# First products of a two-layer network by Strassen's method over pairs of token blocks, weights streamed from DRAM

## The chip, the cores and the metric

The kernel runs on one core of one Trainium2 chip. The metric is device time in microseconds of one execution; less is better. Engine names are those of the profile: PE (TensorE matmul) with PEld (its weight loads), DVE (VectorE), ACT (ScalarE), POOL (GpSimd), SP (SyncE, which here issues every DMA).

## What is computed

Linear attention with an RMS norm gives 4,608 tokens of width 512. Two feed-forward layers follow, each 512 to 2,048 to 512, the first with a scaled squared ReLU, the second with x·sigmoid(1.702x):

```
kv = einsum('bhsd,bhse->bhde', k, v)
out = einsum('bhsd,bhde->bhse', q, kv)
out = out / sqrt(mean(out * out, axis=-1) + 1e-06) * g_norm
x = out.transpose(0, 2, 1, 3).reshape(4608, 512)
h = x @ w1_in;  x = (s * max(h, 0)**2 + b) @ w1_out
h = x @ w2_in;  return (h / (1 + exp(-1.702 * h))) @ w2_out
```

Weights come as float64 and are rebuilt as float32 on the chip. Every large product is made of three float32r matmuls: an operand is split into a high part (`hi`, `gh`, `xh`) and the rest (`lo`, `gl`, `xl`), and high×high, high×low and low×high are summed.

## The kernel before

Tokens stand in nine blocks `j` of 512, the hidden width in sixteen slices `f` of 128, and the layers are `m` = 0 and 1. A step (m, j, f) is two batches of 12 matmuls of 512 columns: `mlp_h` (L255) makes the hidden slice `h` from all 512 inputs, and `mlp_o` (L295), one step later, adds the slice's share to four output banks `o`. Between them `mlp_act` (L263 to L267) and `mlp_g` (L275 to L279) turn `h` into `gh` and `gl` on ACT and DVE. There are 2·9·16 = 288 steps.

Everything else is side work with a due time, called a slot: slot 2i is the `mlp_h` of step i and slot 2i+1 its `mlp_o`, so one slot is one batch of 12 matmuls. The lists at the end of the kernel give each side function its slot: loading and converting weights (`w_load`, `w_low`, `w_words`, `w_hi`, `w_lo`, L82 to L116), the key-value products (`kv_product`, L149, L150), and the attention of the next block (`att_product` L182, `att_mean` L198, `att_newton` L208 to L210, `att_split`). The engines take their instructions in exactly this order. All weights of a layer, high and low, stay in SBUF; those of the second layer are converted during the last block of the first and the first of the second, into the same tiles. PSUM's eight banks are four `o`, two `h` (which the key-value products share) and two for attention.

Of the kernel before, what the change touches and what calls it, by code (L numbers as in the profile page):

```python
# [13 lines left out]
P = 128  # L14
# [13 lines left out]
CONV = [(0, 1, 2, 3), (-0.5, 0, 1, 1.5), (0, 1, 2.5, 4.5)]  # L28
# [3 lines left out]
def kernel(ctx: ExitStack, tc: tile.TileContext, qT, kv_h, kvt, cst,  # L32
# [43 lines left out]
    conv, W = {}, {}  # L76

    def w_load(m, f, which):
        raw = wp.tile([P, 512, 2], U32, tag=f"w{which}_{f}", name="raw")
# [8 lines left out]
        conv[m, f, which] = raw  # L88

    def w_low(m, f, which):  # L90
        raw = conv[m, f, which]
        q = tp.tile([P, 512], U32, tag="ca", name="ca", bufs=4)
        u = tp.tile([P, 512], U32, tag="cu", name="cu", bufs=2)
        act.activation(q, raw[:, :, 0], AF.Copy, scale=2.0 ** -29)
        act.activation(u.bitcast(F32), raw[:, :, 1].bitcast(F32), AF.Abs)
        conv[m, f, which] = (raw, q, u)

    def w_words(m, f, which):
        raw, q, u = conv[m, f, which]
        uf = u.bitcast(F32)  # L100
        dve.tensor_scalar(out=uf, in0=uf, scalar1=ABS_MIN, scalar2=ABS_MAX, op0=ALU.max, op1=ALU.min)  # L101
        dve.tensor_scalar(out=u, in0=u, scalar1=3, scalar2=0x3FFFFFFF, op0=ALU.logical_shift_left, op1=ALU.bitwise_and)  # L102
        dve.scalar_tensor_tensor(out=u, in0=raw[:, :, 1], scalar=SIGN_TOP, in1=u, op0=ALU.bitwise_and, op1=ALU.bitwise_or)  # L103
        dve.tensor_tensor(out=q, in0=u, in1=q, op=ALU.add)  # L104
        conv[m, f, which] = q

    def w_hi(m, f, which):
        a = conv[m, f, which]
        w = wp.tile([P, 2, 512], F32R, tag=f"w{which}_{f}", name=f"w{which}_{f}")
        W[m, f, which] = (w[:, 0, :], w[:, 1, :])  # L110
        act.activation(w[:, 0, :], a.bitcast(F32), AF.Copy)

    def w_lo(m, f, which):
        a = conv.pop((m, f, which))
        hi, lo = W[m, f, which]
        dve.tensor_sub(out=lo, in0=a.bitcast(F32), in1=hi.bitcast(F32))  # L116
# [3 lines left out]
    kvd = [dp.tile([P, NP, D], F32, name=f"kvd{b}") for b in range(B)]  # L120

    def kv_load(b, p):
        if b == 0 and p >= 2:
            t = xp.tile([P, 2, 8, P], F32, tag=("xh", "xl")[p % 2], name="kv_in")
        else:
            t = kp.tile([P, 2, 5, P], F32, tag="kv", name="kv_in")
        nc.sync.dma_start(out=t[:, :, 0:4, :], in_=kv_h[b, p])
        nc.sync.dma_start(out=t[0:D, :, 4, :], in_=kvt[b, p])
        kvin[b, p] = t
# [8 lines left out]
    def q_load(j, p):  # L138
        where = (sp, "s") if j == 0 and p >= 2 else (kp, "q")
        qq = where[0].tile([P, T], F32, tag=where[1], name="qq")  # L140
        for o, n, b, s in segments(j):
            nc.sync.dma_start(out=qq[:, o:o + n], in_=qT[b, p, :, s:s + n])
        qin[j, p] = qq

    def kv_product(b, p, where):
        t = kvin.pop((b, p))
        kv = where[0].tile([P, T], F32, tag=where[1], name="kv")
        for c in range(4):
            pe.matmul(kv[:, :P], lhsT=t[:, 0, c, :], rhs=t[:, 1, c, :], start=(c == 0), stop=False)  # L149
        pe.matmul(kv[:, :P], lhsT=t[0:D, 0, 4, :], rhs=t[0:D, 1, 4, :], start=False, stop=True)  # L150
# [10 lines left out]
        dve.tensor_copy(out=hi, in_=kv[D:P, D:P])  # L161
        if b == 0:
            done.add(("kv", b, p))
# [13 lines left out]
    def att_product(j, p, where):  # L177
        qq = qin.pop((j, p))
        assert all(("kv", b, p) in done for _, _, b, _ in segments(j))
        o_ps = where[0].tile([P, T], F32, tag=where[1], name="o_ps")  # L180
        for o, n, b, s in segments(j):
            pe.matmul(o_ps[:, o:o + n], lhsT=kvbd[b % 2][:, p, :], rhs=qq[:, o:o + n], start=True, stop=True)  # L182
        sq = tp.tile([P, T], F32, tag="t", name="sq")
# [4 lines left out]
        sh = tp.tile([P, T], F32R, tag="t", name="sh")  # L188
        sl = tp.tile([P, T], F32R, tag="t", name="sl")
        act.activation(sh, sq, AF.Copy)  # L190
        dve.tensor_sub(out=sl, in0=sq, in1=sh.bitcast(F32))
        att[j, p] = (o_ps, ones, (sh, sl))

    def att_mean(j, p, where):
        o_ps, mat, parts = att[j, p]
        ms = where[0].tile([P, T], F32, tag=where[1], name="ms")
        for n, sq in enumerate(parts):
            pe.matmul(ms, lhsT=mat, rhs=sq, start=(n == 0), stop=(n == len(parts) - 1))  # L198
        y = tp.tile([P, T], F32, tag="t", name="y")
        y2 = tp.tile([P, T], F32, tag="t", name="y2")  # L200
# [5 lines left out]
    def att_newton(j, p):  # L206
# [3 lines left out]
        dve.scalar_tensor_tensor(out=y2, in0=o_ps, scalar=g_col, in1=y, op0=ALU.mult, op1=ALU.mult)  # L210
        att[j, p] = y2

    def att_split(j, p):
        x = att.pop((j, p))
        if p == 0:
            xT[0, j] = (xp.tile([P, NP, T], F32R, tag="xh", name="xh"), xp.tile([P, NP, T], F32R, tag="xl", name="xl"))
        xh, xl = xT[0, j]
        if j:
            act.activation(xh[:, p, :], x, AF.Copy)  # L219
        else:  # L220
            dve.tensor_copy(out=xh[:, p, :], in_=x)
        pool.tensor_sub(out=xl[:, p, :], in0=x, in1=xh[:, p, :].bitcast(F32))  # L222
# [3 lines left out]
    x2d = [dp.tile([NP, P, T], F32, name=f"x2d{j}") for j in range(NB)]  # L226
    x2in = {}

    def x2_load(j, p):
        t = sp.tile([P, T], F32, tag="s", name="x2")  # L230
        nc.sync.dma_start(out=t, in_=x2d[j][p])
        x2in[j, p] = t

    def x2_split(j, p):
        if p == 0:
            xT[1, j] = (xp.tile([P, NP, T], F32R, tag="xh", name="xh"), xp.tile([P, NP, T], F32R, tag="xl", name="xl"))
        xh, xl = xT[1, j]
        t = x2in.pop((j, p))
        act.activation(xh[:, p, :], t, AF.Copy)  # L239
        pool.tensor_sub(out=xl[:, p, :], in0=t, in1=xh[:, p, :].bitcast(F32))  # L240
        done.add((1, j, p))
# [4 lines left out]
    def mlp_h(m, j, f):  # L246
        xh, xl = xT[m, j]
        wh, wl = W[m, f, 0]
        assert all((m, j, c) in done for c in range(NP))
        h = ps_h.tile([P, T], F32, tag="h", name="h")  # L250
        n = 0
        for c in range(NP):
            cc = slice(c * P, (c + 1) * P)
            for a, x in ((wh, xh), (wh, xl), (wl, xh)):
                pe.matmul(h, lhsT=a[:, cc], rhs=x[:, c, :], start=(n == 0), stop=(n == 3 * NP - 1))  # L255
                n += 1
        G[m, j, f] = h

    def mlp_act(m, j, f):
        h = G[m, j, f]  # L260
        r = gp.tile([P, T], F32, tag="r", name="r")
# [6 lines left out]
        G[m, j, f] = r  # L268

    def mlp_g(m, j, f):  # L270
        r = G[m, j, f]
        gh = gp.tile([P, T], F32R, tag="gh", name="gh")
        gl = gp.tile([P, T], F32R, tag="gl", name="gl")
# [6 lines left out]
        G[m, j, f] = (gh, gl)  # L280

    def mlp_o(m, j, f):
        gh, gl = G.pop((m, j, f))
        wh, wl = W[m, f, 1]
        if f == 0:
            acc[m, j] = [ps_o.tile([P, T], F32, tag=f"o{c}", name=f"o{c}") for c in range(NP)]
        for c in range(NP):
            o = acc[m, j][c]
            cc = slice(c * P, (c + 1) * P)
            if m == 0:  # L290
                pairs = ((wh[:, cc], gh), (wh[:, cc], gl), (wl[:, cc], gh))
            else:
                pairs = ((gh[:, cc], wh), (gh[:, cc], wl), (gl[:, cc], wh))
            for n, (a, x) in enumerate(pairs):
                pe.matmul(o, lhsT=a, rhs=x, start=(f == 0 and n == 0), stop=(f == NF - 1 and n == 2))  # L295

    def mlp_store(m, j):
        for c in range(NP):
            o = acc[m, j][c]
            t = sp.tile([P, T], F32, tag="s", name="st")  # L300
            if c % 2:
                dve.tensor_copy(out=t, in_=o)
            else:
                act.activation(t, o, AF.Copy)
            if m == 0:
                nc.sync.dma_start(out=x2d[j][c], in_=t)
            else:
                nc.sync.dma_start(out=out[j * T + c * P:j * T + (c + 1) * P, :], in_=t)

# [126 lines left out]
```

## Time and profile before

| | |
|---|---|
| median of 3 runs | 1712.54 us (1711.75 to 1712.58) |
| the profiled execution: device time, span of its instructions | 1712.43 us, 1710.6 us |
| PE, DVE, ACT busy in the span | 1685.7 us, 721.9 us, 745.7 us |
| matmuls of PE in the built program | 7,214, of which 3,456 in `mlp_h`, 3,456 in `mlp_o` |
| bytes moved by DMA | 93.22 MB |

Busy time is the sum of an engine's instruction records, and overlapping records of one engine count once. A matmul's record is longer than its pitch, because matmuls are pipelined; the pitch is read from the chain of waits, where a batch is listed with its length. A wait is put down to what came last.

### The profile page before, as it was taken

The page shows a single profiled execution, that of the slowest core. Times are in us where ns is not written, and L with a number is a line of the kernel's source. Part 1 is how long each engine was busy: PE and PEld are TensorE (multiplying, and loading weights), DVE is VectorE, ACT ScalarE, POOL GpSimd, SP SyncE. Part 2 cuts the span into 40 slices and gives each one's busy share as a digit, 9 for nine tenths or more (in the row PEclk, how much of TensorE's full clock was granted, in tenths as well). Part 3 has the DMA queues.
Part 4 walks back from the last instruction along what each step waited for, and adds up shares of the span by engine and source line. Part 5 has one row for each costly group of instructions (what it writes and reads, how often), then busy time and mean ns, then how long its engine had stood idle before and what let it go on. Part 6 is the DMA issues. An engine that isn't in the chain of part 4 may idle for free.

```text
span 1710.6 us, 18774 instructions
## 1 busy us (share of the span) xinstructions
PE 1685.7 (99%) x7460; PEld 1380.0 (81%) x7460; DVE 721.9 (42%) x1110; ACT 745.7 (44%) x1218; POOL 96.1 (6%) x82
## 2 busy tenths in 40 slices
PE   7999999999999999999999999999999999999998
PEld 5877888888888888888877788888888888888887
DVE  5997233433434343434578842222222222222222
ACT  5776455545455454555676532222222222222222
POOL 1000000000000000000000000000000000101000
PEclk8999999999999999999999999999999999999999
DMA  7863401010100001010434110101010101000000
GB/s 239 272 210 104 121 19 46 7 47 7 40 13 32 22 1 53 1 44 7 160 124 164 46 50 1 49 0 48 2 44 7 44 7 38 12 27 24 20 7 25
DMA packets 67655, 93.22 MB, mean 54 GB/s; under 512 B 13808, under 2 KB 40432, under 8 KB 67568
## 3 DMA queue, kind: packets, MB, share of 16 engines
q1 hardware_dynamic: 67568, 92.04, 17.0%
q8 instruction: 58, 0.95, 0.2%
q14 instruction: 29, 0.24, 0.0%
HBM read 72.22 MB, written 19.79 MB: 54 GB/s over the span
## 4 chain that ended last, share of the span: by engine, by line
PE 89%; DVE 7%; DMA 1%; ACT 1%; issue 1%; SPq 0%; DVEq 0%; ACTq 0%
PE o L295 42%; PE h L255 42%; PE o_ps L182 2%; DVE cu L103 1%; PE kv L149 1%; DVE w L116 1%; PE ms L198 1%; DVE ca L104 1%; DVE cu L102 1%; DVE gl L279 1%; DVE cu L101 1%; PE kv L150 1%; DVE r L276 0%; DMA kv_in<-in_kv 0%; DVE r L267 0%
## 5 line engine op out<-in xcount | busy, mean ns | idle before, releaser
L255 PE MATMUL h<-xh,w 128*128 128x512 f32 x2304 | 769.0, 395 | 0.1
L255 PEld LDWEIGHTS h<-xh,w 128*128 128x128 f32 x2304 | 433.2, 188 | 95.0 <-issue 1.7
L255 PE MATMUL h<-xl,w 128*128 128x512 f32 x1152 | 449.0, 390 | 0.0
L295 PE MATMUL o<-gh,w 128*128 128x512 f32 x1152 | 378.2, 389 | 0.0
L295 PE MATMUL o<-w,gh 128*128 128x512 f32 x1152 | 356.2, 390 | 3.4 <-ACT gh L278 3.3
L279 DVE TENSOR_TENSOR gl<-r,gh 128x512 fp32r<-128x512 f32 x288 | 228.9, 795 | 113.6 <-ACT gh L278 100.6
L267 DVE TENSOR_TENSOR r<-h,r 128x512 f32<-128x512 f32 x144 | 99.5, 691 | 414.8 <-ACT r L266 414.8
L266 ACT ACTIVATE r<-h 128x512 f32<-128x512 f32 x144 | 85.8, 596 | 414.8 <-PE h L255 414.7
L295 PEld LDWEIGHTS o<-w,gh 128*128 128x128 f32 x1152 | 216.7, 188 | 49.7 <-ACT gh L278 5.0
L255 PEld LDWEIGHTS h<-xl,w 128*128 128x128 f32 x1152 | 216.8, 188 | 47.7 <-issue 2.7
L295 PEld LDWEIGHTS o<-gh,w 128*128 128x128 f32 x1152 | 216.2, 188 | 45.2 <-ACT gh L275 0.4
L276 DVE TENSOR_SCALAR r<-r,cst_sb 128x512 f32<-128x512 f32 x144 | 78.7, 547 | 379.3 <-ACT gh L275 379.1
L295 PE MATMUL o<-gl,w 128*128 128x512 f32 x576 | 224.9, 390 | 3.7 <-DVE gl L279 3.7
L295 PE MATMUL o<-w,gl 128*128 128x512 f32 x576 | 225.0, 391 | 0.0
L263 ACT ACTIVATE r<-h 128x512 f32<-128x512 f32 x144 | 85.7, 595 | 249.3 <-PE h L255 249.3
L278 ACT ACTIVATE gh<-r 128x512 fp32r<-128x512 f32 x144 | 91.1, 633 | 124.7 <-DVE r L267 124.7
L295 PEld LDWEIGHTS o<-gl,w 128*128 128x128 f32 x576 | 108.1, 188 | 28.8 <-DVE gl L279 6.5
L295 PEld LDWEIGHTS o<-w,gl 128*128 128x128 f32 x576 | 108.3, 188 | 24.1 <-DVE gl L279 1.7
L275 ACT ACTIVATE gh<-r,cst_sb 128x512 fp32r<-128x512 f32 x144 | 117.5, 816 | 4.8
L264 ACT ACTIVATE r<-r 128x512 f32<-128x512 f32 x144 | 91.0, 632 | 4.6
L222 POOL TENSOR_TENSOR xl<-y,xh 128x512 fp32r<-128x512 f32 x36 | 47.6, 1323 | 773.7 <-ACT xh L219 414.0
L240 POOL TENSOR_TENSOR xl<-x,xh 128x512 fp32r<-128x512 f32 x36 | 46.8, 1301 | 698.3 <-ACT xh L239 568.4
(53 smaller groups left out, 846.1 us busy)
## 6 DMA issues: line engine op xcount, KB each, us to landing
raw<-in_w_in SPq DMA_DIRECT2D x32, 512.0 KB, 5.7
kv_in<-in_kv SPq DMA_DIRECT2D x32, 512.0 KB, 4.6
raw<-in_w_out SPq DMA_DIRECT2D x32, 512.0 KB, 6.3
x2d<-st SPq DMA_DIRECT2D x36, 256.0 KB, 2.1
x<-x2d SPq DMA_DIRECT2D x36, 256.0 KB, 2.9
out<-st SPq DMA_DIRECT2D x36, 256.0 KB, 2.1
kv_in<-in_kvt SPq DMA_DIRECT2D x32, 64.0 KB, 4.3
qq<-in_qT SPq DMA_DIRECT2D x8, 256.0 KB, 5.1
```

The costliest lines, as they stand in the source:

```text
L222: pool.tensor_sub(out=xl[:, p, :], in0=x, in1=xh[:, p, :].bitcast(F32))
L240: pool.tensor_sub(out=xl[:, p, :], in0=t, in1=xh[:, p, :].bitcast(F32))
L255: pe.matmul(h, lhsT=a[:, cc], rhs=x[:, c, :], start=(n == 0), stop=(n == 3 * NP - 1))
L263: act.activation(r, h, AF.Relu)
L264: act.activation(r, r, AF.Square)
L266: act.activation(r, h, AF.Sigmoid, scale=1.702)
L267: dve.tensor_mul(out=r, in0=h, in1=r)
L275: act.activation(gh, r, AF.Identity, scale=s_col, bias=b_col)
L276: dve.tensor_scalar(out=r, in0=r, scalar1=s_col, scalar2=b_col, op0=ALU.mult, op1=ALU.add)
L278: act.activation(gh, r, AF.Copy)
L279: dve.tensor_sub(out=gl, in0=r, in1=gh.bitcast(F32))
L295: pe.matmul(o, lhsT=a, rhs=x, start=(f == 0 and n == 0), stop=(f == NF - 1 and n == 2))
```

## The change

Blocks are taken in pairs wherever there are two left: in layer 0, blocks 0 to 2 stay as they were (`plain`), and 3 to 8 form three pairs; in layer 1 blocks 0 to 7 form four pairs and block 8 stays plain. A pair runs in two phases. In the first, `strassen` makes the hidden values of both blocks: for each group `i` of two slices and both halves of the 512 inputs, the 2×2 block product (slices × input halves, by input halves × blocks) is made of seven products of 6 matmuls, in place of eight (two `mlp_h` batches for each of two blocks, 48 matmuls, become 42). In the second phase, `mlp_o` runs as before for both blocks, slice by slice, with eight output banks. The first phase takes 28 slots per pair, and the second 32.

Sums of weight blocks (S1 to S4) are made once per layer (`s_sums`), split, and stored in DRAM (`wsd`) with the plain blocks; both phases load their weights from there (`op_load`, `wo_load`, four slots ahead, `LEAD`). Sums of the inputs are made per pair (`x_operands`) during the second phase before. `g1_sum` joins the seven products, on DVE for five of them. Attention from block 3 on writes its result to DRAM; its units for blocks 5 and 6 stand in the first phase of pair (3, 4), and those of 7 and 8 in that of pair (5, 6). Layer 1's weights are converted in slots 100 to 252, over the three pairs of layer 0. SBUF is 42 slots of 4 KB and 22 of 2 KB per partition, and PSUM eight banks, each given to the next user in the order in which they were freed (`Slots`).

```diff
+NBIG, NMID = 42, 22
+NPLAIN = 3
+LEAD = 4
+OPS = ("A11", "S2", "S3", "S1", "A12", "A22", "S4", "A21")
+PRODUCTS = (("A11", "B11"), ("S2", "T2"), ("S3", "T3"), ("S1", "T1"), ("A12", "B21"), ("A22", "T4"), ("S4", "B22"))
...
+    def op_load(m, i, k):
+        n = min(2, len(PRODUCTS) - 2 * k)
+        t = wl[m, i, k] = new4(F32R, "wl")
+        nc.sync.dma_start(out=t[:, 0:n, :].bitcast(F32), in_=wsd[m][i][:, 2 * k:2 * k + n, :])
...
+    def g1_product(m, i, k):
...
+        for c in range(2):
+            wh, wlo = (w[:, h * 256 + c * P:h * 256 + (c + 1) * P] for h in range(2))
+            xh, xl = (t[:, c, :] for t in x)
+            for a, b in ((wh, xh), (wh, xl), (wlo, xh)):
+                pe.matmul(o, lhsT=a, rhs=b, start=(first and n == 0), stop=(n == 5), skip_group_check=not first)
...
+    def g1_sum(m, i, k):
+        f, f2 = 2 * i, 2 * i + 1
+        if k == 0:
+            st["c1"] = new2(F32, "c1")
+            act.activation(st["c1"], st[0], AF.Copy)
+        elif k == 1:
+            st["u2"] = new2(F32, "u2")
+            dve.tensor_add(out=st["u2"], in0=st[1], in1=st["c1"])
...
+        elif k == 2:
...
+            dve.tensor_add(out=st["u3"], in0=st[2], in1=st["u2"])
+        elif k == 3:
...
+            dve.tensor_add(out=R[f2][:, 1, :], in0=st[3], in1=st["u3"])
+        elif k == 5:
+            dve.tensor_add(out=R[f2][:, 0, :], in0=st[5], in1=st["u3"])
...
+        elif k == 6:
+            dve.tensor_add(out=R[f][:, 1, :], in0=st[6], in1=st["u2"])
...
+    def g1_act(m, i, k):
...
+        if k == 4:
+            R[f] = new4(F32, "r")
+            relu2(m, R[f][:, 0, :], st[4])
...
+        elif k == 3 and m == 1:
+            relu2(m, R[f2][:, 1, :])
+        elif k == 5:
+            if m == 0:
+                relu2(m, R[f2])
+                act.activation(R[f2], R[f2], AF.Square)
+            else:
+                relu2(m, R[f2][:, 0, :])
+        elif k == 6:
+            relu2(m, R[f][:, 1, :])
+            if m == 0:
+                act.activation(R[f], R[f], AF.Square)
...
+    def strassen(m, j, base, shift):
+        for i in range(NF // 2):
+            for k in range(len(PRODUCTS)):
+                slot = base + 3.5 * i + 0.5 * k + (shift if i or k > 1 else 0)
+                at(slot, g1_product, m, i, k)
+                at(slot + 0.52, g1_sum, m, i, k)
+                at(slot + 0.72, g1_act, m, i, k)
+                if k % 2 == 0:
+                    at(slot - LEAD, op_load, m, i, k // 2)
+        base += 28 + shift
+        for f in range(NF):
+            at(base + 2 * f - LEAD, wo_load, m, f)
...
+    for n, j in enumerate(range(NPLAIN + 2, NB, 2)):
+        attend(units(j, j + 1), starts[0][n] + 0.6, 3.2, (0, 1.5, 3, 5))
```

`relu2` is one ACT operation in layer 0, and in layer 1 a sigmoid on ACT followed by a product on DVE.

### The order of instructions

On PE, a step of the kernel before (here in layer 1) opens with the twelve matmuls of `mlp_h` into one bank `h`:

```order
L255 MATMUL h<-xh,w_4_535 128x512
L255 MATMUL h<-xl,w_4_535 128x512
L255 MATMUL h<-xh,w_4_535 128x512 x2
L255 MATMUL h<-xl,w_4_535 128x512
L255 MATMUL h<-xh,w_4_535 128x512 x2
L255 MATMUL h<-xl,w_4_535 128x512
L255 MATMUL h<-xh,w_4_535 128x512 x2
```

In the change, within a first phase of layer 0, the fifth product of a group goes on in bank `a`, the two matmuls of an attention unit follow, and the sixth product takes bank `f`:

```order
L484 MATMUL a<-xh,wl 128x512
L484 MATMUL a<-xl,wl 128x512
L484 MATMUL a<-xh,wl 128x512 x2
L484 MATMUL a<-xl,wl 128x512
L484 MATMUL a<-xh,wl 128x512
L310 MATMUL o_ps<-qq,kvbd_76 128x320
L310 MATMUL o_ps<-qq,kvbd_77 128x192
L484 MATMUL f<-xh,wl 128x512
L484 MATMUL f<-xl,wl 128x512
L484 MATMUL f<-xh,wl 128x512 x2
```

A bank is now done after six matmuls, and each product is read by ACT or DVE at once.

On ACT, an attention unit was spread over three steps of three operations each (`r`, `r`, `gh`); here from a unit's mean (`y`) on:

```order
L201 ACTIVATE y<-ms,eps 128x512
L202 ACTIVATE y<-y 128x512
L203 ACTIVATE y_4560<-y 128x512
L263 ACTIVATE r<-h 128x512
L264 ACTIVATE r<-r 128x512
L275 ACTIVATE gh<-r,cst_sb 128x512
L263 ACTIVATE r<-h 128x512
L264 ACTIVATE r<-r 128x512
L275 ACTIVATE gh<-r,cst_sb 128x512
```

In the change, in the first phase of pair (5, 6), one group of 42 matmuls has between two copies of bank `a` (`c`) an attention unit, half a weight conversion (`ca`, `cu`) and activations of 1,024 columns:

```order
L506 ACTIVATE c_3763<-a 128x512
L136 ACTIVATE ca<-raw 128x512
L137 ACTIVATE cu<-raw 128x512
L313 ACTIVATE sq<-o_ps 128x512
L318 ACTIVATE sh<-sq 128x512
L494 ACTIVATE r<-a 128x512
L494 ACTIVATE r<-r 128x1024
L538 ACTIVATE r<-r 128x1024
L330 ACTIVATE y<-ms,eps 128x512
L331 ACTIVATE y<-y 128x512
L332 ACTIVATE y_3848<-y 128x512
L494 ACTIVATE r<-r 128x512
```

What stood over three steps of 24 matmuls now stands within one group of 42.

On SP, before, layer 0's middle blocks had small loads of `qq` and one store per output slice:

```order
L142 DMA qq<-in_qT 128x192
L142 DMA qq<-in_qT 128x320
L306 DMA x2d_103<-st 128x512 x4
L142 DMA qq<-in_qT 128x256 x2
L172 DMA kvbd_91<-kvd_97 64x4x64
```

In the first phase of pair (5, 6), loads of the product's weights (`wl`), stores of converted weights (`op`, `w`) and of attention results (`y`), and `qq` stand in one queue:

```order
L235 DMA wl<-wsd_3_113 128x1024
L346 DMA x0d_141<-y_5197 128x512
L269 DMA qq<-in_qT 128x512
L235 DMA wl<-wsd_3_113 128x512
L224 DMA wsd_3_121<-op 128x512 x2
L235 DMA wl<-wsd_4_114 128x1024
L130 DMA raw<-in_w_out 128x1024
L235 DMA wl<-wsd_4_114 128x1024 x2
L346 DMA x0d_141<-y_5302 128x512
```

A load of `wl` now stands behind stores that wait for ACT and DVE.

## Rows read from the trace of the kernel before

**Rows 1.** The page: span, and busy time of PE, DVE, ACT.
```profile
span 1710.6 us, 18774 instructions
PE 1685.7 (99%) x7460; PEld 1380.0 (81%) x7460; DVE 721.9 (42%) x1110; ACT 745.7 (44%) x1218; POOL 96.1 (6%) x82
```

**Rows 2.** Chain of waits in layer 1: start us, length us, what.
```profile
1404.32 2.72 PE h L255 x12
1407.04 2.72 PE o L295 x12
...
1456.00 2.72 PE o L295 x12
```

**Rows 3.** Busy time by stretch: length; PE, PEld, DVE, ACT, POOL busy; clock; DMA share; GB/s.
```profile
80.00:120.00 40.00, 37.13 (x174) 28.67 (x173) 38.45 (x67) 28.19 (x52) 3.14 (x2) 1.00 0.72 223
120.00:160.00 40.00, 38.27 (x179) 30.01 (x180) 38.45 (x68) 30.19 (x55) 1.57 (x1) 1.00 0.41 118
...
490.00:655.00 165.00, 165.00 (x730) 135.91 (x729) 66.18 (x90) 86.52 (x133) 10.25 (x8) 1.00 0.09 26
...
820.00:985.00 165.00, 159.56 (x687) 128.74 (x686) 127.43 (x207) 104.89 (x177) 12.13 (x9) 0.99 0.39 128
...
1315.00:1480.00 165.00, 165.00 (x730) 136.67 (x729) 44.94 (x66) 43.74 (x74) 8.99 (x7) 1.00 0.08 26
```

**Rows 4.** Chain of waits around two attention units of layer 0.
```profile
231.63 0.87 PE o_ps L182 x4
232.50 2.75 PE h L255 x12
235.25 2.72 PE o L295 x12
237.97 0.45 PE ms L198 x2
```

**Rows 5.** Groups by shape: count; busy us, mean ns; idle before, releaser (ACT).
```profile
L275 ACT ACTIVATE gh<-r,cst_sb 128x512 fp32r<-128x512 f32 x144 | 117.5, 816 | 4.8
L264 ACT ACTIVATE r<-r 128x512 f32<-128x512 f32 x144 | 91.0, 632 | 4.6
L263 ACT ACTIVATE r<-h 128x512 f32<-128x512 f32 x144 | 85.7, 595 | 249.3 <-PE h L255 249.3
...
L94 ACT ACTIVATE ca<-raw 128x512 uint32<-128x512 uint32 x64 | 42.1, 659 | 3.1 <-DMA raw<-in_w_out 3.1
...
L201 ACT ACTIVATE y<-ms,eps 128x512 f32<-128x512 f32 x36 | 24.7, 687 | 31.7 <-PE ms L198 31.7
...
L158 ACT ACTIVATE kvs<-kv 64x64 f32<-64x64 f32 x28 | 5.8, 208 | 24.4 <-PE kv L150 24.4
```

**Rows 6.** Groups by shape, DVE and ACT in layer 1, 1315 to 1645 us.
```profile
L266 ACT ACTIVATE r<-h 128x512 f32<-128x512 f32 x61 | 36.4, 597 | 196.7 <-PE h L255 196.7
...
L279 DVE TENSOR_TENSOR gl<-r,gh 128x512 fp32r<-128x512 f32 x61 | 42.3, 693 | 42.6 <-ACT gh L278 42.6
L267 DVE TENSOR_TENSOR r<-h,r 128x512 f32<-128x512 f32 x61 | 42.2, 692 | 194.2 <-ACT r L266 194.2
```

**Rows 7.** DMA: two stretches of 5 and one of 40 us, as in rows 3.
```profile
935.00:940.00 5.00, 4.87 (x21) 3.39 (x20) 3.02 (x5) 3.24 (x6) 0.89 (x1) 1.00 1.07 381
940.00:945.00 5.00, 4.62 (x21) 3.44 (x19) 4.83 (x9) 1.27 (x3) 0.41 (x1) 1.00 1.07 375
...
40.00:80.00 40.00, 39.92 (x194) 32.32 (x194) 36.22 (x68) 32.38 (x60) 0.00 (x0) 1.00 0.89 276
```

**Rows 8.** DMA issues, 40 to 80 us: count, size, median us to landing.
```profile
raw<-in_w_in SPq DMA_DIRECT2D x6, 512.0 KB, 7.9
raw<-in_w_out SPq DMA_DIRECT2D x5, 512.0 KB, 7.2
```

**Rows 9.** Chain of waits, 820 to 1000 us: one load by itself.
```profile
833.24 3.96 DMA raw<-in_w_out
```

More of the change, by code (lines that the diff above doesn't have):

```diff
@@ L227 @@
[L227 to L241, printed above, removed]
+    xin, xop = {}, {}
@@ new lines, in x_load, with x_hi, x_lo @@
+    def x_load(m, j, k):
+        assert all((m, j, 2 * k + n) in done for n in range(2))
+        t = xin[m, j, k] = new4(F32, "x")
+        nc.sync.dma_start(out=t, in_=xd[m][j][2 * k:2 * k + 2].rearrange("k p t -> p k t"))
+    def x_hi(src, key):
+        hi, lo = xop[key] = new4(F32R, "xh"), new4(F32R, "xl")
+        act.activation(hi, xin[src], AF.Copy)
+    def x_lo(src, key, last):
+        hi, lo = xop[key]
+        dve.tensor_sub(out=lo, in0=xin[src], in1=hi.bitcast(F32))
+        if last:
+            drop(xin.pop(src))
@@ L336, with attention, plain @@
-    pa, pb = (ps_a, "pa"), (ps_a, "pb")
+    def attention(slots, j, p):
+        for slot, fn in zip(slots, (att_product, att_mean, att_newton, att_split)):
+            at(slot, fn, j, p)
+    def plain(m, j, base, last):
+        for f in range(NF):
+            at(base + 2 * f, mlp_h, m, j, f)
+            at(base + 2 * f + 1, mlp_act, m, j, f)
+            if f:
+                at(base + 2 * f + 1, mlp_o, m, j, f - 1)
+                if last:
+                    at(base + 2 * f + 1, wo_done, m, f - 1)
+            at(base + 2 * f + 1.01, mlp_g, m, j, f)
+        end = base + 2 * NF + 1
+        at(end - 0.01, mlp_o, m, j, NF - 1)
+        if last:
+            at(end - 0.01, wo_done, m, NF - 1)
+        at(end + 0.02, mlp_store, m, j)
@@ L339, with x_done @@
+    def x_done(m, left):
+        drop(*(xin.pop(k) for k in left))
     for p in range(NP):
[L340 removed]
+        kv_work(-99 + p, START[p][0], 0, p)
         at(-99 + p, q_load, 0, p)
[L342 removed]
+        attention(START[p][1:], 0, p)
     weight(-128, -58.5, 3.5, CONV[0], 0, 0, 0)
     weight(-89, -48.5, 4, CONV[0], 0, 1, 0)
[L347 removed]
@@ L365 @@
-    for j in range(NB):
-        for p in range(NP):
-            slot = 2 * NF * (NB + j - 1) + 1 + 3.5 * p
-            at(slot, x2_load, j, p)
-            at(slot + 3, x2_split, j, p)
-    for n in range(2 * NF):
-        slot = 2 * NF * (NB - 1) + 3 + 1.75 * n
-        weight(slot - 3, slot, 1, CONV[2], 1, n // 2, n % 2)
-    side.sort(key=lambda e: e[:2])
-    side.reverse()
-    def run(end):
-        while side and side[-1][0] < end:
-            _, _, fn, a = side.pop()
-            fn(*a)
+        kv_work(2 * n - 8.9, 2 * n - 5, 1 + n // NP, n % NP)
@@ new lines @@
+    for j in range(NPLAIN):
+        plain(0, j, 32 * j, j == NPLAIN - 1)
+    base = 32 * NPLAIN
+    seconds = {0: [], 1: []}
+    starts = {0: [], 1: []}
+    for j in range(NPLAIN, NB, 2):
+        starts[0].append(base)
+        seconds[0].append(strassen(0, j, base, j == NPLAIN))
+        base = seconds[0][-1] + 32
+    half = base
+    for j in range(0, NB - 1, 2):
+        starts[1].append(base)
+        seconds[1].append(strassen(1, j, base, 0))
+        base += 60
+    plain(1, NB - 1, base, True)
@@ new lines, in attend, with units @@
+    def attend(units, first, step, gaps):
+        for u, (j, p) in enumerate(units):
+            slot = first + step * u
+            if p == 0 and j < B:
+                at(slot - 2.2, kvbd_load, j)
+            at(slot - 4, q_load, j, p)
+            attention([slot + i for i in gaps], j, p)
+    def units(*blocks):
+        return [(j, p) for j in blocks for p in range(NP)]
+    attend(units(1), 7, 6, (0, 2, 4, 6))
+    attend(units(2, 3), 34, 3.7, (0, 1.5, 3, 4.5))
+    attend(units(4), 65, 3, (0, 1.5, 3, 4.5))
@@ L382 @@
+    for f in range(NF):
+        at(base + 2 * f - LEAD, wi_load, 1, f)
+        at(base + 2 * f + 2 - LEAD, wo_load, 1, f)
+    events.sort(key=lambda e: e[:2])
     with tc.manual_schedule():
```

459 lines of the change are left out of this document (332 added, 127 removed).

## The prediction

> **What bounds the kernel now.** I read the page first: PE is busy for 1685.7 of 1710.6 us, DVE and ACT for 42 and 44% [rows 1]. Busy records overlap, so I took PE's pitch from the chain of waits. There batches of twelve matmuls follow one another at exactly 2.72 us, `h` then `o`, with nothing between, and ten batches lie between the second and the third row shown [rows 2]. A matmul so takes 2.72 / 12 = 0.2267 us, and one slot is 2.72 us. The table by stretch tells whether this holds everywhere. In the middle of each layer it does: 165 us with PE busy throughout and 730 matmuls, in layer 0 with ACT at 86.5 us and DVE at 66.2 [rows 3]. It fails in two places, and DVE is the fullest engine beside PE in both. From 80 to 160 us, where weights are converted under the first block, DVE is busy for 76.9 of 80 us and PE for 75.4; from 820 to 985 us, where the layers change, only 687 matmuls are recorded instead of 730 [rows 3]. So PE bounds nearly all of the run, and what takes matmuls away pays in full, as long as ACT, DVE and the queue of SP keep ahead.
>
> **What is removed.** Seven pairs of 8 groups each save 6 matmuls per group: 7·8·6 = 336 matmuls, and 336·0.2267 = **76.2 us** [rows 2]. They all stood on the path. The seven products use the same tiles of 128 weights by 512 columns, so I keep the pitch; that six matmuls and not twelve go to one bank leaves the `o` batches as a model, which put three matmuls on each of four banks at the same 2.72 us. The loss at the change of layers should also go: 730 − 687 = 43 matmuls, 43·0.2267 = **9.7 us** [rows 3]. Layer 1's conversions now end at slot 252, and layer 1 begins at slot 277. The loss from 80 to 160 us stays, because the conversions of slots 0 to 32 keep their places: 4.6 us, already in the old time. Key-value products and attention keep their matmuls; a unit costs PE 0.87 + 0.45 = 1.32 us [rows 4], before as after.
>
> **What is added on ACT and DVE.** The place to look is the first phase of pairs (3, 4) and (5, 6), where products, eight attention units and layer 1's conversions meet. PE needs 28·2.72 + 8·1.32 = 86.7 us there. ACT's work, with durations of [rows 5]: an activation of 1,024 columns is not in the trace. Its ends are one instruction of 512 (632 ns) and two (1264). From 64 to 512 columns the time goes from 208 to 595 ns, 0.86 ns per column, so 512 more columns give 632 + 442, about 1.07 us, which I take. A group then has a copy (0.6), a ReLU from PSUM (0.6), two ReLUs and two squares, of which three have 1,024 columns (3·1.07 + 0.63): 5.04 us, times eight 40.3. An attention unit has `sq`, `sh`, the logarithm, the exponential and a square: 0.6 + 3·0.63 + 0.69 = 3.18, times eight 25.4. Conversions give six pairs of 0.66 (7.9), eight operand splits and two `w` splits of 0.63 (6.3). Two stores of 0.6 and the first scalings and splits of phase two (2·1.26 + 3·0.63) add 5.6. The sum is **85.5 us against PE's 86.7**, 98%. At 1264 ns per wide activation it is 90, at 632 ns 75. DVE has per group five sums (28 us in all), per unit `sl` and three operations of `att_newton` (22 us), and 46 operations of conversion, splitting and storing, many of them shorter; all at the 0.69 us of [rows 6] that is at most 28 + 22 + 32 = 82 us, 94%.
>
> An engine that full costs PE something. The one measured case is 80 to 160 us: DVE 96% busy, PE 94%, so 5.8% lost [rows 3]. For 87 us that is 5 us, and **10 us** for both stretches. Bounds: nothing, if ACT's lag is worked off in phase two, where it has, for sixteen slices, 1.26 + 2·0.63 each, with 7 splits of inputs and some 12 us of conversions 60 us of work for 87; and if ACT and DVE wait on one another so that ACT reaches only 80% of a stretch, 85.5 / 0.8 = 107 us, 20 us too many each and 40 together. I stand near the lower end, because the row is a full engine in this same program.
>
> Elsewhere these engines have room. In the other phases of layer 0 ACT and DVE have, by the same count, 45 to 75% of PE's time. In layer 1 a group of 9.52 us has on DVE five sums and four products with the sigmoid, 9·0.69 = 6.2 us [rows 6], and on ACT a copy and four sigmoids, 3.0 us. The inputs' sums and splits (18 operations of 1,024 columns per pair) stand in phase two, beside `gl` and `gh`. Where phases change, the first product or the first `o` takes a bank that ACT or DVE must empty, 0.6 to 0.7 us each, while PE has a batch of 2.72 us to do; at 14 changes that costs between nothing and two evictions each (18 us). With the full last slots before block 3 I take **5 us**, about a third, since the batch covers the first two evictions.
>
> **What is added on SP and DMA.** A group loads 3.5 tiles of 512 KB, 1.84 MB in 9.52 us: 193 GB/s. In the two full stretches conversions, `qq` and attention results bring this to about 26 MB in 87 us, 295 GB/s. The trace shows 375 and 381 GB/s for 5 us each and 276 over 40 us, with PE busy for 39.92 of the 40 [rows 7]. Loads of 512 KB landed 7.2 to 7.9 us after issue there [rows 8], and they are issued four slots ahead, 10.9 us. So I cost the streaming at nothing; its cover is the 3 us that are left. SP issues in order, and a load of `wl` is queued behind stores that wait for ACT and DVE. When ACT falls more than 3 us behind, PE waits for its weights too, and this is within the 40 us above.
>
> The rule that speaks against the change is the Trainium skill's, "DMA: Bandwidth & Descriptors", sections "Anatomy of one DMA" and "Bandwidth": a DMA has about 2.0 us fixed, plus bytes over 436 GB/s, and transfers should be 1 MiB or more. An estimate by that page is 3.2 us for 512 KB, so loads in turn would move 164 GB/s, a group would take 12.2 us, and the sum would end near 1790. This case's trace doesn't agree, for the loads overlap: 276 GB/s times 7.9 us is 2.2 MB in flight [rows 7, 8].
>
> **The sum.** 1710.6 − 76.2 − 9.7 + 10 + 5 = 1639.7 us of span. The profiled execution took 1.8 us more than its span (1712.43), and it stands 0.1 us from the median. **Forecast: 1642 us**, 4.1% faster.
>
> **The rivals.**
> *ACT bounds the two full stretches.* For it: 98% by the budget, with DVE at up to 94% and each waiting for the other within a unit (`sh` for `sl`, the square for `att_newton`). Against: before, ACT and DVE were never both this full. Its price is 40 instead of 10: 1672 us.
> *The saving is given back in layer 1's groups.* DVE does a product only after ACT's sigmoid of the sum just made, 0.6 us that DVE spends idle, four times per group: 6.2 + 2.4 = 8.6 of 9.52 us [rows 6]. If it then runs over by 0.5 to 1 us in each of 32 groups, that is 16 to 32 us: about 1666. Against: sums become ready at intervals of 1.36 us, so much of the wait falls where DVE has nothing to do.
> *Loads come late* in every group by up to 1 us, for example because stores hold SP up also outside the full stretches: up to 56 us, 1665 to 1698.
> *Slower: the streamed loads run one after another.* One alone took 3.96 us [rows 9], so a group's three and a half take 13.9, which is 4.4 us too long, 56 times: some 245 us, 1885. It decides from the point where the loss reaches 70 us, 1.25 us per group, which is a delivery under 170 GB/s. Against it stand the 276 GB/s.
> *The change does not do what it says:* the built program has 6,878 matmuls where 7,214 were, so the 336 are gone. What could fail is the pitch alone; 3% more of it in the products would take 16 us.
>
> **How the numbers follow.** Forecast with its small stalls (1622 to 1655): 0.60. ACT-bound stretches: 0.17. Layer 1's groups: 0.10. Late loads, still faster: 0.05. Losses that just cancel the gain: 0.03. Slower: 0.05. A measurement of this kernel can tell 0.2% (3.4 us) from no change, and the cases above give faster 0.92, same 0.03, slower 0.05. The lowest time has no new stall at all and a start without its 4.6 us: 1710.6 − 76.2 − 9.7 − 4.6 + 1.8 = 1622. Upward the range takes in ACT's 40 us, with half of layer 1's or the late loads' price on top: 1685.
>
> **What would show it.** Right: the chain of waits has batches of six matmuls at 1.36 us in the first phases; layer 1's stretches have PE busy throughout, with 42 matmuls in 9.5 us; the layers change without a gap; the lost time sits at about slots 96 to 125 and 157 to 185, on waits for ACT. Wrong: waits of PE on DMA of `wl`, or a layer-1 pair that takes more than 60·2.72 = 163 us, or a full stretch over 100 us.

## The result and the profile after

The changed kernel takes 1668.53 us (median of 4 runs, 1668.09 to 1668.77) where the kernel before took 1712.47: a ratio of 0.9744 (0.9727 to 0.9761). It is 44 us faster, where 70 were forecast. The profiled execution has a span of 1666.9 us instead of the forecast 1639.7, so 27.2 us are to be found. The time lies inside the stated range, 1622 to 1685, but above the branch that the forecast stood on (1622 to 1655) and close to the price of a rival (1672).

The page of the changed kernel, its lines for the span and the engines [rows 1]:

```profile
span 1666.9 us, 19740 instructions
PE 1619.2 (97%) x7124; PEld 1317.3 (79%) x7124; DVE 943.5 (57%) x1485; ACT 816.7 (49%) x1273; POOL 18.2 (1%) x22
```

PE's share fell from 99 to 97%: idle time has appeared. The busy time by stretch (columns as in rows 3) says that it isn't in layer 1. The first four rows are of layer 0's pairs, the last of layer 1:

```profile
400.00:420.00 20.00, 16.09 (x61) 12.73 (x61) 10.23 (x18) 13.10 (x19) 0.00 (x0) 0.83 0.73 227
420.00:440.00 20.00, 16.81 (x72) 12.80 (x70) 11.25 (x19) 14.24 (x23) 0.00 (x0) 1.00 0.71 259
440.00:460.00 20.00, 17.01 (x72) 13.14 (x73) 13.82 (x23) 13.96 (x21) 0.00 (x0) 1.00 0.87 301
640.00:660.00 20.00, 15.95 (x55) 11.68 (x54) 11.76 (x21) 13.73 (x20) 0.00 (x0) 0.83 0.50 170
...
900.00:1060.00 160.00, 160.00 (x708) 132.48 (x707) 84.24 (x119) 52.68 (x84) 0.00 (x0) 1.00 0.48 171
```

How long each phase took is read from the timeline of PE, from its first matmul to the first of the next phase (`a` opens a first phase, `o` a second one):

```profile
371.35 0.39 PE L484 MATMUL a<-xh,wl 128*128 128x512 f32 x1
...
480.03 0.40 PE L441 MATMUL o<-gh,w 128*128 128x512 f32 x1
567.09 0.39 PE L484 MATMUL a<-xh,wl 128*128 128x512 f32 x1
...
669.14 0.39 PE L441 MATMUL o<-gh,w 128*128 128x512 f32 x1
756.18 0.39 PE L484 MATMUL a<-xh,wl 128*128 128x512 f32 x1
836.05 0.39 PE L441 MATMUL o<-gh,w 128*128 128x512 f32 x1
923.09 0.39 PE L484 MATMUL a<-xh,wl 128*128 128x512 f32 x1
999.25 0.39 PE L441 MATMUL o<-w,gh 128*128 128x512 f32 x1
```

A layer-1 first phase takes 999.25 − 923.09 = 76.16 us, which is 28·2.72 to the hundredth; all four do. Second phases take 87.04 to 87.06 us, 32·2.72. In layer 0, pair (5, 6) needs 669.14 − 567.09 = 102.05 us and pair (3, 4), which begins at 371.35 and has one last `o` batch of the block before in it, 480.03 − 371.35 − 2.72 = 105.96. The forecast without stalls was 86.7 for each. Pair (7, 8) takes 79.87 instead of 76.16. That a full stretch takes over 100 us is one of the prediction's own signs of being wrong.

The chain of waits in a layer-1 first phase has the batches that were forecast, six matmuls in 1.36 us [rows 2]:

```profile
995.33 1.36 PE a L484 x6
996.69 1.36 PE f L484 x6
```

PE's waits, over the whole run (engine, what it was to write, line, for whom: us in total, times, longest):

```profile
PE a L484 <- ACT c L506: 13.2, 10, 3.9
PE d L484 <- DVE r L517: 11.8, 11, 2.2
PE h L397 <- DVE kvs L288: 9.4, 7, 2.0
```

All three are new: in the kernel before, the longest entry of this list was 3.7 us, and none was of `h`. The fifth product goes on in bank `a`, which ACT must have copied (`c`), and the seventh in bank `d`, which DVE must have read. No wait is for a load of `wl`: these, 168 of 512 KB, landed 7.4 us after issue (median), and 20 us of layer 1 in which DMA moved 407 GB/s have PE busy for 20.00:

```profile
1260.00:1280.00 20.00, 20.00 (x90) 16.57 (x89) 12.64 (x19) 6.25 (x11) 0.00 (x0) 1.00 1.03 407
```

### One wait, followed back

The longest of these waits ended at 408.20 us. PE's timeline there:

```profile
403.90 0.39 PE L484 MATMUL d<-xh,wl 128*128 128x512 f32 x1
408.20 0.79 PE L484 MATMUL a<-xh,wl 128*128 128x512 f32 x1 [3.91 <-ACT c L506]
408.79 0.63 PE L484 MATMUL a<-xl,wl 128*128 128x512 f32 x1
409.22 1.05 PE L484 MATMUL a<-xh,wl 128*128 128x512 f32 x2
410.07 0.63 PE L484 MATMUL a<-xl,wl 128*128 128x512 f32 x1
410.50 0.63 PE L484 MATMUL a<-xh,wl 128*128 128x512 f32 x1
```

ACT's timeline before it:

```profile
398.30 0.58 ACT L494 ACTIVATE r<-a 128x512 f32<-128x512 f32 x1
401.49 1.06 ACT L494 ACTIVATE r<-r 128x1024 f32<-128x1024 f32 x1 [2.61 <-DVE r L519]
402.58 1.06 ACT L538 ACTIVATE r<-r 128x1024 f32<-128x1024 f32 x1
403.54 0.61 ACT L212 ACTIVATE op<-ca 128x512 fp32r<-128x512 f32 x1
404.06 0.61 ACT L494 ACTIVATE r<-r 128x512 f32<-128x512 f32 x1
404.71 1.06 ACT L544 ACTIVATE r<-r 128x1024 f32<-128x1024 f32 x1
405.67 0.67 ACT L330 ACTIVATE y<-ms,eps 128x512 f32<-128x512 f32 x1
406.37 0.63 ACT L331 ACTIVATE y<-y 128x512 f32<-128x512 f32 x1
407.03 0.63 ACT L332 ACTIVATE y<-y 128x512 f32<-128x512 f32 x1
407.57 0.58 ACT L506 ACTIVATE c<-a 128x512 f32<-128x512 f32 x1
```

The copy `c` at 407.57 needs only bank `a`, but it stands behind nine operations, and the second of these had waited 2.61 us for DVE's sum `r` (L519). DVE's timeline says why that sum was late, and what the copy then cost DVE:

```profile
396.00 0.68 DVE L517 TENSOR_TENSOR r<-d,u 128x512 f32<-128x512 f32 x1
396.60 0.68 DVE L337 SCALAR_TENSOR_TENSOR y<-ms,y 128x512 f32<-128x512 f32 x1
...
400.43 0.42 DVE L204 TENSOR_TENSOR s<-ca,s 128x256 f32<-128x256 f32 x1
400.77 0.68 DVE L519 TENSOR_TENSOR r<-f,u 128x512 f32<-128x512 f32 x1
401.37 0.68 DVE L217 TENSOR_TENSOR op<-ca,op 128x512 fp32r<-128x512 f32 x1
401.97 0.68 DVE L522 TENSOR_TENSOR r<-d,u 128x512 f32<-128x512 f32 x1
408.18 0.69 DVE L509 TENSOR_TENSOR u<-b,c 128x512 f32<-128x512 f32 x1 [5.53 <-ACT c L506]
```

Between its sums DVE did a Newton step, `sl` and four weight sums. While it caught up, ACT stood idle; while ACT caught up, DVE stood idle for 5.53 us, and PE for 3.91. Neither engine is full: in the rows from 400 to 460 us above, ACT is busy for 13.1 to 14.2 and DVE for 10.2 to 13.8 of 20 us. Afterwards PE's matmuls of 512 columns follow one another at 0.43 us instead of 0.2267, from 408.79 to 410.93, with a granted clock of 0.83 over those 20 us.

The whole first phase of pair (3, 4), in the same columns, with that last `o` batch in it:

```profile
371.35:480.03 108.68, 95.51 (x398) 74.61 (x396) 70.71 (x118) 74.98 (x112) 0.00 (x0) 0.97 0.73 251
```

So the theory at this point: the two stretches lose their time to the order in which ACT and DVE take instructions on which PE waits, each engine being idle much of the time. The rival is the prediction's: there is too much work in them.

### The profile page after: what moved, and what is told of

Read it like the earlier page. It is cut to its first block, busy times and chain, and to the rows that moved or that the text cites. A ratio compares the mean times of both kernels' runs of the same rounds, so it can differ in the third digit from the quotient of the medians.

```text
span 1666.9 us, 19740 instructions
## 1 busy us (share of the span) xinstructions
PE 1619.2 (97%) x7124; PEld 1317.3 (79%) x7124; DVE 943.5 (57%) x1485; ACT 816.7 (49%) x1273; POOL 18.2 (1%) x22
## 4 chain that ended last, share of the span: by engine, by line
PE 58%; DVE 1%; ACT 0%; DMA 0%; issue 0%; SPq 0%; DVEq 0%
PE o L441 34%; PE d L484 6%; PE a L484 6%; PE f L484 3%; PE c L484 3%; PE b L484 3%; PE h L397 3%; DMA x<-x1d 0%; ACT r L494 0%; DVE r L517 0%; ACT r L538 0%; DVE u L513 0%; DVE r L519 0%; DVE u L509 0%; DVE cu L149 0%
## 5 line engine op out<-in xcount | busy, mean ns | idle before, releaser
L555 DVE TENSOR_TENSOR gl<-r,gh 128x512 fp32r<-128x512 f32 x224 | 150.2, 687 | 156.2 <-ACT gh L551 154.1
L397 PE MATMUL h<-xh,w 128*128 128x512 f32 x512 | 173.5, 400 | 9.7 <-DVE kvs L288 9.4
L484 PE MATMUL a<-xh,wl 128*128 128x512 f32 x448 | 159.8, 397 | 13.2 <-ACT c L506 13.2
L484 PE MATMUL d<-xh,wl 128*128 128x512 f32 x448 | 158.5, 394 | 11.8 <-DVE r L517 11.8
L397 PEld LDWEIGHTS h<-xh,w 128*128 128x128 f32 x512 | 96.5, 188 | 36.7 <-DVE kvs L288 14.0
L452 DVE COPY st<-o 128x512 f32<-128x512 f32 x36 | 24.7, 690 | 164.7 <-PE o L441 164.6
L484 PEld LDWEIGHTS a<-xh,wl 128*128 128x128 f32 x448 | 85.1, 190 | 35.4 <-ACT c L506 17.9
L484 PEld LDWEIGHTS d<-xh,wl 128*128 128x128 f32 x448 | 84.1, 188 | 33.9 <-DVE r L517 16.6
L499 DVE TENSOR_TENSOR r<-r,t 128x512 f32<-128x512 f32 x96 | 66.5, 693 | 70.3 <-ACT t L498 70.3
L397 PE MATMUL h<-xl,w 128*128 128x512 f32 x256 | 100.3, 392 | 1.9 <-POOL xl L359 1.9
L484 PE MATMUL a<-xl,wl 128*128 128x512 f32 x224 | 88.2, 394 | 0.0
```

The lines of the kernel that those rows point to most:

```text
L397: pe.matmul(h, lhsT=a, rhs=b, start=(n == 0), stop=(n == 3 * NP - 1))
L484: pe.matmul(o, lhsT=a, rhs=b, start=(first and n == 0), stop=(n == 5), skip_group_check=not first)
L499: dve.tensor_mul(out=r, in0=src, in1=t)
L555: dve.tensor_sub(out=gl, in0=R[f][:, n, :], in1=gh.bitcast(F32))
```

## The experiments

### Activations behind the copy

```diff
+LATE = 1.0
...
-                at(slot + 0.72, g1_act, m, i, k)
+                at(slot + 0.72 + (LATE if m == 0 and k > 4 else 0), g1_act, m, i, k)
```

> Layer 0's ReLU and squares of the sixth and seventh product are put one slot later in the order (so behind the next group's copy of bank a on ACT); nothing else moves and no work is added or removed. In the changed kernel the first phases of pairs (3,4) and (5,6) take 106.0 and 102.1 us where PE alone needs 86.7. If the loss is one of order (ACT stands in front of a ReLU that waits for DVE, while the copy that PE and DVE wait for is queued behind it), most of it goes: both phases at 88 to 95 us, the time at 1640 to 1653. If ACT is simply full (98% by its budget), order does not help: phases over 100 us, time at 1664 to 1672.

1655.05 us (1652.58 to 1657.41), 0.9668 (0.9652 to 0.9684). No instruction was taken away, and 13 us went. Pair (3, 4) took 93.93 us, pair (5, 6) still 100.48. PE's waits for `c`, 13.2 us before, are gone, and those on bank `d` have grown:

```profile
PE d L485 <- DVE r L518: 13.6, 9, 3.7
```

In the first pair ACT and DVE did the same work as before, busy for 74.5 and 70.9 us, in 12 us less. The order was the cause on ACT's side. In the second pair the sum on DVE took the copy's place. Only the first pair met what was expected of the order; the time is 2 us above that range, and the second pair stayed over the 100 us expected of a full ACT. The profiled run was the fastest of the four, so its phases belong to 1652.58 us.

### Conversions spread evenly

Layer 1's conversions before ended at slot 252, and stood densely in the two stretches.

```diff
-    slot = 32 * NPLAIN + 4
     for i in range(NF // 2):
+        slot = (127, 143, 187, 202, 217, 232, 247, 262)[i]
...
-        slot += 9
+        slot += 7
...
-            slot += 5
+            slot += 4
```

> Layer 1's weight conversions leave the first phases of pairs (3,4) and (5,6) and stand in the second phases and the first phase of pair (7,8). That takes some 14 us of ACT and 26 us of DVE out of each full stretch (ACT from 98% to about 82% of PE's time, DVE from at most 94% to 65%). If load is the cause, the two stretches fall to 88 to 92 us, and the time to 1636 to 1645, unless the new places lose what is won. If order is the cause, about half stays: stretches of 95 to 100 us, 1650 to 1658.

1651.28 us, 0.9641 (0.9627 to 0.9655). The stretches took 94.86 and 94.16 us. PE still waited 6.2 us on `d` and 4.7 on `a`. Fewer instructions in front of the copy and the sum shorten the queue there, without ending it. The time is the one expected if order is the cause, and the stretches lie just under that range. The run doesn't separate order from load, though: it also took work out of the stretches (ACT was busy for 64.2 us of the first instead of 75.0, DVE for 51.9 instead of 70.7).

### Both together

> The two edits together: layer 0's late ReLUs and squares one slot later, and layer 1's conversions out of the two full stretches. By each alone the first phase of pair (3,4) went from 106.0 to 93.9 (order) and 94.9 us (conversions), that of pair (5,6) from 102.1 to 100.5 and 94.2; what was left after the first edit were two waits of 3.7 us behind a burst of conversions on DVE. If order and bursts on DVE are two causes that add, both stretches come to 87 to 90 us and the time to 1631 to 1640. If what is left in each is the same thing (attention's own chains between ACT and DVE), the stretches stay at 92 to 94 and the time at 1643 to 1650.

1641.92 us (1640.92 to 1644.51), 0.9588 (0.9574 to 0.9602). Stretches of 89.66 and 93.07 us, and pair (7, 8) at 76.16. The waits on `a` are no longer in the list, and those on `d` are down to

```profile
PE d L485 <- DVE r L518: 6.3, 4, 3.7
```

The edits mostly add: 13.5 and 17.3 us alone, 26.6 together. So they act mostly on different waits. The first stretch came into the range expected of two causes that add, the second into that of the rival, and the time lies between the two.

### Attention in step with the groups

In the version with both edits one wait of 3.69 us on `d` was left, at 647 us. On DVE a Newton step stood in front of the sum: attention units come every 3.2 slots and groups every 3.5, so the step falls into another place of each group.

```diff
-        attend(units(j, j + 1), starts[0][n] + 0.6, 3.2, (0, 1.5, 3, 5))
+        attend(units(j, j + 1), starts[0][n] + (1.6 if n == 0 else 0.6), 3.5, (0, 1.5, 3, 5))
```

> The kernel of e5_both, with the attention units of the two full stretches 3.5 slots apart in place of 3.2, so one unit to each group of 42 matmuls, always at the same place in it: the Newton step (three operations on DVE) then always comes right behind the sum of the seventh product, and no longer in front of it in some groups. Theory that the loss left (89.7 and 93.1 us against 86.7) is still the order on DVE in front of that sum: PE's waits d <- DVE r of 6.3 us go under 2, the two stretches take 87 to 89 us, and the time is 1634 to 1638. Rival, that what is left is the conversions' own work beside attention (ACT and DVE waiting on one another, whatever the order): the waits move to another bank, the stretches stay at 89 to 93, and the time is 1640 to 1644. Slower, by over 1646, if the last unit, which now ends 1.5 slots into the second phase, holds up the inputs of the next pair there.

1637.07 us (1636.95 to 1637.95), 0.9561 (0.9548 to 0.9574): the fastest version, 31 us under the changed kernel, and all three numbers expected by the theory of order came true. The stretches took 87.43 and 87.88 us against 86.7 without a stall. PE's longest waits now:

```profile
PE h L398 <- DVE kvs L289: 9.5, 7, 2.0
PE kv L276 <- DMA kv_in<-in_kv: 3.4, 2, 2.9
PE o L442 <- DVE y L340: 2.4, 2, 1.2
```

Banks `a` and `d` are gone from them. The third row is new: the last attention unit reaches into the second phase, which waits for its bank, and the two second phases take 89.14 and 89.10 us instead of 87.04. For the second pair both phases together went from 180.11 to 176.98 us; for the first they stayed (176.70 and 176.57).

### Half of the key-value copies to ACT

These three experiments are on the third wait, `h` for `kvs`, in the first block. `h` takes the PSUM bank that a key-value product has held, once DVE has copied it out. Here the second copy of each product goes from DVE to ACT.

```diff
         if b:
             act.activation(lo, kv[0:D, 0:D], AF.Copy)
+            act.activation(hi, kv[D:P, D:P], AF.Copy)
         else:
             dve.tensor_copy(out=lo, in_=kv[0:D, 0:D])
-        dve.tensor_copy(out=hi, in_=kv[D:P, D:P])
+            dve.tensor_copy(out=hi, in_=kv[D:P, D:P])
```

> Both copies of a key-value product stand on ACT; before, the second was on DVE. In the first block of the changed kernel PE's h waited 9.4 us, seven times, for DVE to empty a bank that a key-value product had held. If DVE's queue (over 85% busy there) is what makes the bank late, the waits fall to under 3 us and the time by 5 to 9, to 1660 to 1664. If ACT is as late as DVE because it waits for DVE's conversions itself, the wait only changes its name: 1666 to 1672.

1668.60 us, 0.9742 (0.9727 to 0.9756): no change, as expected if the wait only changes its name. The wait was divided among others, and their sum, 9.0 us, is nearly the 9.4 of before:

```profile
PE h L398 <- ACT kvs L286: 5.4, 7, 1.1
PE o L442 <- DVE gl L425: 3.6, 7, 0.9
```

### A PSUM bank for the key-value products alone

On top of both edits, one bank is kept for these products, so that `h` never takes it.

```diff
+    def kv_bank():
+        if not kvfree:
+            return psum("kv")
...
-        kv = psum("kv")
+        kv = kv_bank()
...
-        drop(kv)
+        kv_drop(b, p, kv)
```

> As e5_both, and key-value products keep one PSUM bank of their own, so that h never takes a bank that DVE has still to empty. If the order in which banks are handed out is the cause of the 9.4 us, the waits of h for kvs are gone and the time is 5 to 9 us under e5_both. If DVE's load is the cause, PE waits elsewhere instead (key-value products for their own bank, o for gl): within 3 us of e5_both.

1645.67 us, 0.9609 (0.9593 to 0.9625): 3.8 us slower than without, outside both expectations. The wait of `h` for `kvs` is gone, and has two successors:

```profile
PE kv L292 <- DVE kvs L305: 7.8, 2, 7.2
PE h L414 <- ACT r L426: 6.7, 7, 1.4
```

The wait of 7.2 us stands before the first `h`, which starts at 38.37 us instead of 28.02, because several products now follow one another through one bank. Yet block 1 starts at 166.87 us, 2.5 before the version without the bank, whose clock was lower there, and 1.8 behind the version with attention in step, whose clock from 80 us on was 1.00 too. So something was won inside the first block and given back ahead of it; what the order of banks costs, this run doesn't tell.

### Subtractions of the first block's conversions to POOL

On top of both edits.

```diff
-        dve.tensor_sub(out=w[:, 1, :], in0=q.bitcast(F32), in1=w[:, 0, :].bitcast(F32))
+        eng = pool if u[0] == 0 and u[1] > 1 else dve
+        eng.tensor_sub(out=w[:, 1, :], in0=q.bitcast(F32), in1=w[:, 0, :].bitcast(F32))
```

> As e5_both, and layer 0's low weight parts (slices 2 to 15) are made on POOL instead of DVE: some 20 us of DVE's work in the first block goes to an idle engine. If DVE's load makes the key-value banks late, PE's 9.4 us of waits for them fall below 3 and the time is 5 to 10 us under e5_both. If POOL's 1.3 us each slow DVE down instead, or ACT's chain takes over as in the run that moved the copies, it is within 3 us of e5_both.

1653.20 us, 0.9652 (0.9637 to 0.9666): 11 us slower, outside both expectations. DVE has 25 instructions fewer from 60 to 160 us and yet is busy for 88.9 us instead of 82.8, and PE's wait for `kvs` grew from 9.2 to 13.8 us. The groups of DVE and POOL by shape in that stretch, with the subtraction on POOL:

```profile
L150 DVE SCALAR_TENSOR_TENSOR cu<-raw,cu 128x512 uint32<-128x512 uint32 x22 | 26.0, 1182 | 0.8
...
L426 DVE TENSOR_TENSOR gl<-r,gh 128x512 fp32r<-128x512 f32 x10 | 10.0, 999 | 0.4
L167 POOL TENSOR_TENSOR w<-ca,w 128x512 fp32r<-128x512 f32 x22 | 31.9, 1453 | 47.9 <-ACT w L161 47.9
```

The same two groups with it on DVE:

```profile
L150 DVE SCALAR_TENSOR_TENSOR cu<-raw,cu 128x512 uint32<-128x512 uint32 x23 | 15.9, 693 | 0.8
...
L425 DVE TENSOR_TENSOR gl<-r,gh 128x512 fp32r<-128x512 f32 x11 | 7.6, 693 | 0.4
```

### Loads issued two slots ahead instead of four

```diff
-LEAD = 4
+LEAD = 2
```

> Streamed weights are asked for two slots (5.4 us) ahead instead of four; loads of 512 KB landed 7.4 us after issue in the changed kernel. If a load is issued at its slot, PE waits about 2 us for the loads of each group in all seven first phases and for w in the second: 100 us and more slower, over 1760. If SP runs ahead of the slots, because buffers come free early, there is little to see: 1668 to 1690, with waits for DMA on PE.

1672.40 us (two runs), 0.9765 (0.9745 to 0.9784), 3.9 more than the changed kernel and in the range expected if SP runs ahead. Layer 1 stayed at 76.16 us per first phase (76.45 once), although two slots are 5.4 us and a load takes 7.4 to land. So the slot of a load isn't the time of its issue. The traces show SP ahead of it: from the issue of a load of `wl` to the first matmul that uses it passed 18 to 31 us in the changed kernel (medians of the phases), and still 13 to 26 us here. The least time from landing to use was 4.1 us there, and 0.04 us here, so a lead of two leaves nothing over. In PE's list only 1.6 us of waits for `w` are new, and they stand in layer 1's last block, which takes 2.2 of the 3.9 us more.

## Why the prediction was right in sign and 27 us short

**What is removed.** It came out to the hundredth: layer 1's first phases of 76.16 us are 42 matmuls per group at the old pitch, and 336 matmuls are worth the 76.2 us. (Between the second and the third row of [rows 2] lie 17 batches, not ten; the pitch is the same.) The layers change without a gap: layer 1 begins at 923.09 us, and PE is busy throughout from 900 to 1060. From 820 to 985 us 718 matmuls are recorded where 687 were [rows 3]; what lacks to a full 730 lacks before 836 us, in pair (7, 8), which runs at its full pitch in the versions with both edits.

**What is added on ACT and DVE.** This is the step that failed: "An engine that full costs PE something", 5 us per stretch. The stretches lost 105.96 − 86.7 = 19.3 and 102.05 − 86.7 = 15.4 us, 34.7 instead of 10. The durations under it were right: a ReLU of 1,024 columns took 1.06 us (taken: 1.07), the wide scaling 1.23 (1.26). Their sum was too high: ACT was busy for 75.0 and 73.4 us in the two stretches and not 85.5, DVE for 70.7 and 69.6 where at most 82 were counted. Records of one engine overlap (ACT's add up to 80.2 us in the first), and five of its operations, 4.4 us, slid past the end. With them ACT had work for some 91% of PE's 86.7 us, not 98%. The size even met the upper bound, "if ACT and DVE wait on one another so that ACT reaches only 80%", 20 us each. I had named the mechanism and then stood at the other end, "because the row is a full engine in this same program". That row [rows 3, 80 to 160 us] is of one engine that is 96% busy and so hardly waits. Here two in-order engines feed one another, and PE stands behind both. A budget of busy time can't price that; the runs did. With the work unchanged, one move of the activations took 13.5 us out. It left 13.8 us in the second stretch; how much of these is order and how much load, the runs don't divide, since the spread of the conversions changed both. With the conversions spread and attention in step, 1.9 of the 34.7 us are left inside the stretches, and some 4.2 more have moved to the second phases.

The rival "ACT bounds the two full stretches", at 1672, had the place and nearly the time. It was wrong in the cause: ACT is busy for two thirds of the worst windows, and not 98%. The waits that PE's list has there are not the whole loss: those on `a` and `d` come to 25.0 us in all three pairs, which lost 38.4 together, and 11.8 of these 25.0 are for DVE. Part of the other 13.4 is the pitch of 0.43 us after long waits; I didn't divide up the rest.

**Elsewhere.** "I take 5 us" should have been about 10. Pair (7, 8) lost 3.7 us by the same order: the move of the activations alone takes it to 76.96, both edits to 76.16. The rest lies before block 3: its first product starts at 371.35 us, where the kernel before had its first `h` of block 3 at 359.31:

```profile
359.31 0.39 PE L255 MATMUL h<-xh,w 128*128 128x512 f32 x1
```

Four attention units done earlier (4·1.32 = 5.3) explain less than half, and some 6.7 us are new. Of these 4.2 are lost before block 1 begins (164.41 instead of 160.26 us), 1.2 in block 1 and 1.4 in block 2, where PE's list has next to nothing. PE was busy for 72.8 us from 80 to 160 where it had been for 75.4, so "The loss from 80 to 160 us stays … already in the old time" was 2.6 us short; from 40 to 80 us, where nothing had been lost, it was 37.7 instead of 39.9. The longest listed wait there is that of `h` for `kvs`, and three attempts on it gained nothing. That banks are now passed on in the order in which they come free may be behind it; this was only argued.

**The sum again.** 24.7 us more in the stretches and 5.4 elsewhere make 30.1; the miss is 27.2. The 2.9 us in between, in my favour, are losses of the kernel before that were larger than counted. There the layers changed with a loss of 10.8 us, not 9.7: block 8 of layer 0 and block 0 of layer 1 lasted from 822.16 to 1007.04 us, for 2·87.04 us of matmuls, and the row counted only to 985. Its blocks 3 to 7 took 1.3 us more than their matmuls with four units each, and it had 0.6 us more behind its last matmul.

**SP and DMA.** Costed at nothing, and nothing it was; the rivals of late loads, of loads one after another and of layer 1's groups fall with the exact 76.16 us. The estimate of 12.2 us per group, from the Trainium skill, "DMA: Bandwidth & Descriptors", section "Anatomy of one DMA", is not borne out: a group takes 9.52 us, with DMA at up to 407 GB/s. There the Trainium skill gives its 2.0 us and its rate for one transfer on GpSimd's path. That loads follow one another was added in the estimate; here SP issues them, and 512 KB that land 7.4 us after issue, at up to 407 GB/s, overlap.

## What to carry to other kernels

A product that goes on in a bank which another engine has to read first makes that reader part of PE's chain: give the reading its own early place in the queue of its engine, and let long side work come right behind it. Before a stretch is priced by busy shares, list for each instruction on which PE waits what stands in front of it on its engine, and what that in turn waits for; two engines that are each busy for two thirds of a stretch can stop a third. Side work that repeats should have the period of the loop it stands in, so that it is in a good place every time and not only in some.

## What the runs showed of the hardware

A wait can cost more than its length. Behind the 3.91 us above, matmuls came at 0.43 us for more than 2 us, near twice 0.2267 as the two levels of 2.4 and 1.2 GHz would have it; the granted clock of that window was 0.83. The same happened behind a wait of 2.87 us at 646 us, but not behind one of 3.69 us in the version with both edits, where the clock stayed at 1.00 and the third matmul was back at the old pitch. Behind the same wait, 3.71 us, in the version with a bank of its own for `kv` the clock fell to 0.91, and the second phase that follows took 88.67 us instead of 87.04. So the length of the one wait doesn't decide it. In the first block the clock differed between executions whose waits were alike: with both edits PE was granted 0.91 to 0.92 from 80 to 140 us, in the changed kernel and with attention in step 1.00, with the same wait of 9.2 to 9.5 us for `kvs`. Block 3 then began at 376.21 instead of 371.35 and 372.03 us. Of the 7.4 us between the spans of the profiled executions with both edits and with attention in step, 4.2 so lie before block 3, and 3.1 in the second pair. Their medians are 4.9 us apart, so some 1.8 of these may be the clock's; the 3.1 are the order's.

POOL at work stretched DVE's instructions: with the subtractions on POOL, the means rose from 693 to 1182 and to 999 ns with two inputs from SBUF, and for an operation with one tensor input (L423 in that version) from 544 to 716. A mean mixes two kinds. From 40 to 160 us of that run, the operation at L150 took 692 ns in the 16 cases with no POOL instruction beside it and 1773 in the 11 with one; `gl` took 692 and 1375. Not every operation beside POOL is stretched: two of the six `gl` kept their 693 ns, and three Newton steps 692. The Trainium skill, "SBUF — State Buffer", section "Who interferes with whom", says that DVE shares a pair of ports with GpSimd as an exclusive lock, and that an instruction with two SBUF inputs contends for it with one of GpSimd that reads SBUF. The two with two inputs from SBUF agree with that. The third (L423) agrees only if that operation runs in the two-port mode which the same section names; no run here shows in which it ran.
